# GpSimd's weight arithmetic in 128-column pieces, and w_out staged in a place of its own

## The chip, the core and the metric

The kernel runs on one core of a Trainium2 chip. The metric is the device time of one execution in microseconds (us), and a kernel's time is the median over several executions. Engines have short names in what follows: PE is TensorE, PEld its weight loads, DVE is VectorE, ACT is ScalarE, POOL is GpSimd, and SP is SyncE, which here only issues DMA transfers. Every engine works through its own instructions in a fixed order and waits where an operand or a place to write is not ready.

## The reference, cut

A linear attention without softmax, normalised per head, feeds a gated layer with a spatial product. There are 8 batches, 8 heads, 576 positions and 64 channels per head.

```python
kv  = einsum('bhsd,bhse->bhde', k, v)
out = einsum('bhsd,bhde->bhse', q, kv)
x   = out / sqrt(mean(out**2, -1) + 1e-6) * g_norm      # (B, S, 512)
h   = maximum(x @ w_in, 0);  u, v = h[..., :512], h[..., 512:]
v_n = (v - mean(v)) / sqrt(var(v) + 1e-6)
v_s = einsum('ts,bsd->btd', w_spatial, v_n) + b_spatial[None, :, None]
result = (u * v_s) @ w_out
```

## The kernel before

Operands of the large products are split into a high and a low part (XH and XL, WIH and WIL, WSH and WSL, VH and VL, GH and GL, WOH and WOL), and each product is three products: high by high, high by low, low by high (`three`, L223). One batch goes through these stages.

- Attention, a pair of heads at a time: `att_k` (K, tile `pskv`), `att_qa` and `att_qb` (Q, tiles `pso` and `pst`, the normalised result `x`), `att_t` (T, transposition into `pstr`, from which ACT writes XH and DVE writes XL). The last 64 positions of all pairs go through `pstt`. All these PSUM tiles but `pst` share three places (`ps_att`).
- `hv` (tile `psh`): the second half of x @ w_in for 128 positions, then the layer norm on ACT and DVE, which gives VH and VL. `hv_tail` does this for the last 64 positions of two batches and writes TA and TB.
- `u_unit` (tile `psu`): a 128-channel, 288-position piece of the first half of x @ w_in, written to U by ACT.
- `sp_unit` (tile `pss`): the spatial product, which DVE multiplies with U into `g` (L298). ACT writes GH and DVE writes GL.
- `out_unit` (tile `pso2`): the last product, copied out by ACT and stored.

The weights arrive as 64-bit numbers. `weight64` (L343) decodes one 128x512 piece: ACT L348, DVE L349 and L350, ACT L351 (the high part), DVE L352 and L353, then POOL L354 (a subtraction) and L355 (an addition that writes the low part). There are eight pieces of w_in and four of w_out. The spatial weights need one ACT cast and one POOL subtraction of 640 columns each (`make_ws`, L376), and their last rows need two of each per half (`make_tail`, L393). Staged pieces live in the pool `stage0` (five places), the first four in `stage1`.

The first batch, the attention of the second, all weight loads (token W) and all decodes (token C) are written in one list of tokens, PLAN. After it, batches 1 to 7 run in a loop: hv, u, spatial, out. A scheduler orders the instructions of each engine from this program order as operands come free, so that an engine's order differs from the order of the code. The attention of later batches is queued in steps (`queue`, `step`) between the units.

Of the kernel before, what the change touches and what calls it, by code (L numbers as in the profile page):

```python
# [13 lines left out]
ALU = mybir.AluOpType  # L14
AX = mybir.AxisListType

B, H, S, D = 8, 8, 576, 64
DM, FF = 512, 1024
FH = FF // 2
P = 128  # L20
# [13 lines left out]
HALF = DM // 2  # L34
NB = B
PLAN = """
N8 W L J00 D00 L W G J01 B00 C A01 L W L J02 T00 C H30 W B01 C D02 J03 H10 W C T01 L B02 C W
T02 H20 D03 H11 L L L W C L K10 B03 L C H00 T03 H21 d0 W H12 H22 b0 W H31 J11 t0 H01 D10 H13
+ J12 W C W A11 B10 K13 C H23 u00 W A12 H32 A13 H02 W u01 u31 F1 u21 u30 u10 L C B11 W C W
F2 W u20 B12 u11 H03 H33 W T11 d1 F3 S T10 T12 F0 S C C b1 C t1 W C B13 S C T13 h C C s30  # L40
s31 s11 s21 s00 s20 s01 S s10 o1 S o3 S S S S S S o0 S o2
"""


def f32(ap):
    return ap.bitcast(F32)
# [3 lines left out]
def body(ctx: ExitStack, tc, qT, kvlo, kvhi, g2, w_in, wsT, bsp, w_out, out):  # L50
    nc = tc.nc
# [12 lines left out]
    def persistent(shape, dt, name):  # L64
        return const.tile(shape, dt, name=name, tag=name)
# [4 lines left out]
    WSH = persistent([P, NC, WC], F32R, "WSH")  # L70
    WSL = persistent([P, NC, WC], F32R, "WSL")
    WTH = persistent([P, WC], F32R, "WTH")
    WTL = [persistent([P, WC], F32R, f"WTL{i}") for i in range(2)]
# [134 lines left out]
    def att_steps(b):  # L208
        st = {}

        def t2():
            att_t(b, 2, st)
            tail_a(b, st)
            tail_b(b, st)

        K = lambda p: (lambda: att_k(b, p, st))
        Q = lambda p: (lambda: att_q(b, p, st))
        T = lambda p: (lambda: att_t(b, p, st))
        return [K(0), K(1), Q(0), K(2), Q(1), T(0), K(3), Q(2), T(1), Q(3), t2, T(3),
                lambda: att_tail(b, st)]  # L220


    def three(ps, pairs):  # L223

        n = len(pairs)
        for i, (lt, rh) in enumerate(pairs):
            nc.tensor.matmul(ps, lt, rh, start=i == 0, stop=i == n - 1)  # L227

    def hl(lh, ll, rh, rl):
        return [(lh, rh), (lh, rl), (ll, rh)]  # L230
# [17 lines left out]
    def hv(b, c):  # L248
        ps = ps_ho.tile([P, 512], F32, name="psh", tag="ho")
        for k in range(NP):  # L250
            hv_k(b, c, k, ps)
        hv_end(c, ps, nc.vector)
# [12 lines left out]
    def hv_tail():  # L265
        ps = ps_ho.tile([P, 512], F32, name="psh", tag="ho")
        cols = slice(NT, NT + 2 * TAIL)
        three(ps, [m for k in range(NP) for m in
                   hl(XH[:, k, cols], XL[:, k, cols], WIH[:, k, FH:FF], WIL[:, k, FH:FF])])
        v = layer_norm(ps, nc.vector)  # L270
        for i in range(2):
            own = slice(i * TAIL, (i + 1) * TAIL)
            other = slice((1 - i) * TAIL, (2 - i) * TAIL)
            nc.scalar.copy(TA[i][own], v[own])
            nc.vector.tensor_copy(TB[i][own], v[own])
            nc.vector.tensor_tensor(TA[i][other], v[own], f32(TA[i][own]), op=ALU.subtract)

    def u_unit(b, d, j):
        ps = ps_us.tile([P, 512], F32, name="psu", tag="us")
        cols = slice(j * HS, (j + 1) * HS)  # L280
        xs = slice(b % 2 * S + j * HS, b % 2 * S + (j + 1) * HS)
        fs = slice(d * P, (d + 1) * P)
        three(ps[:, 0:HS], [m for k in range(NP) for m in
                            hl(WIH[:, k, fs], WIL[:, k, fs], XH[:, k, xs], XL[:, k, xs])])
        nc.scalar.activation(U[:, d, cols], ps[:, 0:HS], AF.Relu)  # L285

    def sp_unit(b, d, j):
# [18 lines left out]
        for src, dst in parts:  # L306
            nc.scalar.copy(GH[:, d, dst], g[:, src])  # L307
            nc.vector.tensor_tensor(GL[:, d, dst], g[:, src], f32(GH[:, d, dst]), op=ALU.subtract)

    def out_unit(b, c):  # L310
        ps = ps_ho.tile([P, 512], F32, name="pso2", tag="ho")
        cols = slice(c * P, (c + 1) * P)
        three(ps, [m for k in range(4) for m in
                   hl(GH[:, k, cols], GL[:, k, cols], WOH[:, k, :], WOL[:, k, :])])
        o = work.tile([P, DM], F32, name="o", tag="stg", bufs=2)
# [11 lines left out]


    GH = GL = WOH = WOL = None
    staging = [ExitStack(), ExitStack()]  # L330
    pools = [staging[0].enter_context(tc.tile_pool(name="stage0", bufs=5)),
             staging[1].enter_context(tc.tile_pool(name="stage1", bufs=4, side="right"))]
    staged = {}

    def stage(i, n, dt=F32):
        pool = pools[1 if i < 4 else 0]
        staged[i] = pool.tile([P, 2 * DM], dt, name="stage", tag="stage")[:, 0:n]
        return staged[i]

    def load64(src, i):  # L340
        nc.sync.dma_start(stage(i, 2 * DM, U32), src)

    def weight64(i, hi, lo):  # L343

        wide = staged.pop(i).rearrange("p (f two) -> p f two", two=2)
        w0, w1 = wide[:, :, 0], wide[:, :, 1]
        t = work.tile([P, DM], U32, name="t", tag="stg", bufs=2)
        nc.scalar.activation(f32(t), f32(w1), AF.Abs, scale=2.0 ** -112)  # L348
        nc.vector.tensor_scalar(t, t, 3, None, op0=ALU.logical_shift_left)  # L349
        nc.vector.scalar_tensor_tensor(w1, w1, 0x80000000, t, op0=ALU.bitwise_and, op1=ALU.bitwise_or)  # L350
        nc.scalar.copy(hi, f32(w1))  # L351
        nc.vector.tensor_scalar(t, w1, 0xFF800000, None, op0=ALU.bitwise_and)  # L352
        nc.vector.scalar_tensor_tensor(f32(w0), w0, 2.0 ** -52, f32(t), op0=ALU.mult, op1=ALU.mult)  # L353
        nc.gpsimd.tensor_tensor(f32(w1), f32(w1), f32(hi), op=ALU.subtract)  # L354
        nc.gpsimd.tensor_tensor(lo, f32(w1), f32(w0), op=ALU.add)  # L355

    def w_in_cols(half):
        return slice(half * FH, (half + 1) * FH)
# [14 lines left out]
    def load_ws(c, i):  # L373
        nc.sync.dma_start(stage(i, WC), wsT[c * P:(c + 1) * P, :])

    def make_ws(c, i):  # L376
        t = staged.pop(i)
        nc.scalar.copy(WSH[:, c, :], t)
        nc.gpsimd.tensor_tensor(WSL[:, c, :], t, f32(WSH[:, c, :]), op=ALU.subtract)

    def tail_rows(i):
        h0 = (1 - i) * TAIL
        return slice(i * TAIL, (i + 1) * TAIL), slice(h0, h0 + TAIL), h0, h0 + 32

    def load_tail(i, slot):

        rows, rest, h0, h1 = tail_rows(i)
        t = stage(slot, WC)
        nc.sync.dma_start(t[rows], wsT[NC * P:S, :])
        for r in (h0, h1):  # L390
            nc.sync.dma_start(t[r:r + 1], bsp)

    def make_tail(i, slot):  # L393
        rows, rest, h0, h1 = tail_rows(i)
        t = staged.pop(slot)
        nc.gpsimd.memset(f32(WTL[i][rest]), 0.0)
        nc.gpsimd.memset(f32(TB[i][rest]), 0.0)
        for r in (h0, h1):
            nc.gpsimd.memset(f32(TB[i][r:r + 1]), 1.0)
        nc.scalar.copy(WTH[rows], t[rows])  # L400
        nc.gpsimd.tensor_tensor(WTL[i][rows], t[rows], f32(WTH[rows]), op=ALU.subtract)
        for r in (h0, h1):
            nc.scalar.copy(WTL[i][r:r + 1], t[r:r + 1])
        low = WTL[i][h1:h1 + 1]
        nc.gpsimd.tensor_tensor(low, t[h1:h1 + 1], f32(low), op=ALU.subtract)


    todo = [(b, p) for b in range(B) for p in range(NP)]
# [9 lines left out]
    def ahead(n=1):  # L418
        wanted[0] += n
        issue()  # L420
# [17 lines left out]
    def enqueue(b):  # L438
        for i, s in enumerate(att_steps(b)):
            def go(i=i, s=s):  # L440
                s()
                if i in (2, 4, 7, 9):
                    ahead()
            queue.append(go)

    def step(n=1):
        for _ in range(n):
            if queue:
                queue.pop(0)()

    def spatial(b, d, j):
        nonlocal GH, GL
        if GH is None:
            staging[0].close()
            gates = ctx.enter_context(tc.tile_pool(name="gates", bufs=1))
            GH, GL = (gates.tile([P, 4, NT + 2 * TAIL], F32R, name=n, tag=n)
                      for n in ("GH", "GL"))
        sp_unit(b, d, j)
# [6 lines left out]
    loads = [lambda ld=ld, args=args, n=n: ld(*args, n) for n, (ld, mk, args) in enumerate(jobs)]  # L465
# [28 lines left out]
    for token in PLAN.split():  # L494
        do[token[0]](*map(int, token[1:]))

    for b in range(1, NB):
        for c in range(NC):
            hv(b, c)
            step()  # L500
        for d in range(4):
            if d == 3 and b % 2 == 0:
                step(len(queue))
                hv_tail()
            for j in range(2):
                u_unit(b, d, j)
                step()
        step(len(queue))
        if b + 2 < NB:
            enqueue(b + 2)  # L510
        for d in range(4):
            for j in range(2):
                sp_unit(b, d, j)
                step()
        for c in ([NC] if b % 2 else []) + list(range(NC)):
            out_unit(b, c)
            step()


_OUTS = [((B, S, DM), "float32")]  # L520
# [41 lines left out]
```

## Time and profile before

| | us |
|---|---|
| median of three runs | 553.45 (552.96 to 555.08) |
| the profiled execution, its own time | 550.85 |
| its span, first to last instruction | 549.1 |
| PE busy in the span | 524.3 |
| DVE busy | 312.6 |
| ACT busy | 220.1 |
| POOL busy | 51.8 |

The profiled execution is 2.6 us shorter than the median, so a change is worked out against the profiled execution and then carried over to the median. PE is busy nearly all the time after the first 97 us. In the first 97 us, which load and decode the weights, PE has gaps, and DVE has almost none from 20 us on. All of POOL's work lies in the first 88 us.

### The profile page before, as it was taken

What the parts mean: (1) busy time and instruction counts of PE and PEld (TensorE: products, weight loads), DVE (VectorE), ACT (ScalarE), POOL (GpSimd) and SP (SyncE); (2) the same over time, 40 slices, a digit from 0 to 9 for tenths busy, and PEclk for the clock granted to TensorE, in tenths of its full rate; (3) what the DMA queues carried; (4) which work ended last, traced back from release to release, by engine and by line L of the source; (5) the groups of instructions that cost most, each with busy time, mean ns of one, the idle gap of its engine ahead of it and who ended that gap; (6) DMA issues with size and microseconds to landing.
All of it is one profiled execution on the core that took longest, in us unless ns stands there. A gap on an engine that the chain in (4) does not pass through costs nothing.

```text
span 549.1 us, 8840 instructions
## 1 busy us (share of the span) xinstructions
PE 524.3 (95%) x3344; PEld 480.0 (87%) x3344; DVE 312.6 (57%) x871; ACT 220.1 (40%) x576; POOL 51.8 (9%) x50
## 2 busy tenths in 40 slices
PE   7787978999999999999999999999999999999996
PEld 6666966988998889988999889988999889988995
DVE  1999999813565465555364465646546456314530
ACT  3766955422434343243433344334332434123312
POOL 6356643000000000000000000000000000000000
PEclk9999899999999999999999999999999999999999
DMA  8999835111244103430333202431100200010002
GB/s 227 288 278 227 271 90 140 33 39 39 69 104 125 59 0 89 112 116 20 87 88 84 100 1 65 109 108 55 44 23 1 78 20 1 0 47 32 1 1 96
DMA packets 20034, 46.26 MB, mean 84 GB/s; under 512 B 2644, under 2 KB 3156, under 8 KB 19992
## 3 DMA queue, kind: packets, MB, share of 16 engines
q1 hardware_dynamic: 19992, 45.70, 30.0%
q8 instruction: 26, 0.43, 0.3%
q14 instruction: 16, 0.13, 0.1%
HBM read 36.25 MB, written 9.44 MB: 83 GB/s over the span
## 4 chain that ended last, share of the span: by engine, by line
PE 82%; DVE 3%; ACT 0%; issue 0%; ACTq 0%; DVEq 0%
PE pss L227 21%; PE pso L227 18%; PE psu L227 16%; PE psh L258 14%; PE pskv L110 4%; PE pso L165 4%; PE pstr L195 2%; PE psh L227 1%; PE pst L170 1%; PE pstt L203 0%; DVE stage L353 0%; DVE ss L151 0%; DVE XL L189 0%; DVE x L157 0%; DVE rh L133 0%
## 5 line engine op out<-in xcount | busy, mean ns | idle before, releaser
L227 PE MATMUL pss<-WSH,VH 128*128 128x288 f32 x256 | 78.8, 308 | 1.3 <-DVE g L298 1.3
L227 PE MATMUL psu<-XH,WIH 128*128 128x288 f32 x256 | 77.6, 303 | 0.3 <-ACT U L285 0.3
L227 PE MATMUL psu<-XL,WIH 128*128 128x288 f32 x256 | 76.1, 298 | 0.0
L227 PE MATMUL psu<-XH,WIL 128*128 128x288 f32 x256 | 76.0, 298 | 0.0
L227 PE MATMUL pss<-WSH,VL 128*128 128x288 f32 x256 | 75.5, 295 | 0.0
L227 PE MATMUL pss<-WSL,VH 128*128 128x288 f32 x256 | 75.4, 295 | 0.0
L307 ACT CAST GH<-g 128x288 fp32r<-128x288 f32 (+2 forms) x80 | 29.0, 382 | 83.3 <-DVE g L298 83.2
L227 PE MATMUL pso<-WOH,GH 128*128 128x512 f32 x144 | 58.8, 408 | 0.4 <-ACT o L320 0.4
L227 PE MATMUL pso<-WOL,GH 128*128 128x512 f32 x144 | 56.8, 395 | 0.0
L227 PE MATMUL pso<-WOH,GL 128*128 128x512 f32 x144 | 56.8, 398 | 0.0
L237 DVE BATCH_NORM_STATS2 s<-v 128x6 f32<-128x512 f32 x36 | 24.8, 692 | 52.5 <-ACT v L234 52.5
L298 DVE TENSOR_TENSOR g<-pss,U 128x288 f32<-128x288 f32 x64 | 29.1, 456 | 44.8 <-PE pss L227 44.2
L258 PE MATMUL psh<-WIH,XH 128*128 128x512 f32 x128 | 51.0, 398 | 0.5 <-ACT XH L188 0.5
L227 PEld LDWEIGHTS psu<-XH,WIH 128*128 128x128 f32 x256 | 48.8, 191 | 1.5 <-ACT U L285 0.4
L258 PE MATMUL psh<-WIL,XH 128*128 128x512 f32 x128 | 50.1, 391 | 0.0
L227 PEld LDWEIGHTS pss<-WSH,VH 128*128 128x128 f32 x256 | 48.2, 188 | 2.0 <-DVE g L298 1.5
L227 PEld LDWEIGHTS psu<-XL,WIH 128*128 128x128 f32 x256 | 48.7, 190 | 1.2
L227 PEld LDWEIGHTS psu<-XH,WIL 128*128 128x128 f32 x256 | 48.7, 190 | 0.8
L258 PE MATMUL psh<-WIH,XL 128*128 128x512 f32 x128 | 48.6, 392 | 0.2 <-DVE XL L189 0.2
L110 PE MATMUL pskv<-KV 128*128 128x128 f32 x320 | 45.6, 282 | 3.2 <-DMA KV<-kvhi 3.0
L227 PEld LDWEIGHTS pss<-WSL,VH 128*128 128x128 f32 x256 | 48.2, 188 | 0.4
L227 PEld LDWEIGHTS pss<-WSH,VL 128*128 128x128 f32 x256 | 48.0, 188 | 0.0
(100 smaller groups left out, 982.0 us busy)
## 6 DMA issues: line engine op xcount, KB each, us to landing
KV<-kvlo SPq DMA_DIRECT2D x31, 320.0 KB, 4.5
qt<-qT SPq DMA_DIRECT2D x32, 288.0 KB, 3.9
out<-o SPq DMA_DIRECT2D x32, 256.0 KB, 2.0
KV<-kvhi SPq DMA_DIRECT2D x31, 256.0 KB, 4.0
stage<-w_in SPq DMA_DIRECT2D x8, 512.0 KB, 10.3
stage<-w_out SPq DMA_DIRECT2D x4, 512.0 KB, 6.6
stage<-wsT SPq DMA_DIRECT2D x4, 320.0 KB, 12.3
out<-o SPq DMA_DIRECT2D x8, 128.0 KB, 2.3
```

What stands on the lines that cost most here:

```text
L110: nc.tensor.matmul(ps[:, 0:P], kv[:, 0, c, :], kv[:, 1, c, :], start=c == 0, stop=c == NC)
L165: nc.tensor.matmul(ps[:, c * P:(c + 1) * P], qt[:, c * P:(c + 1) * P], kvb, start=True, stop=True)
L170: nc.tensor.matmul(st["tail"][:, p * P:(p + 1) * P], qt[:, S - P:S], kvb, start=True, stop=True)
L195: nc.tensor.transpose(ps[:, c * P:(c + 1) * P], x[:, c * P:(c + 1) * P], ident)
L227: nc.tensor.matmul(ps, lt, rh, start=i == 0, stop=i == n - 1)
L237: nc.vector.bn_stats(s6, v)
L258: nc.tensor.matmul(ps, lt, rh, start=k == 0 and i == 0, stop=k == NP - 1 and i == 2)
L298: nc.vector.tensor_tensor(g, ps[:, 0:HS], U[:, d, cols], op=ALU.mult)
L307: nc.scalar.copy(GH[:, d, dst], g[:, src])
```

## The change

Every POOL subtraction and addition of the weights is cut into pieces of 128 columns (`pieces`): a 128x512 instruction becomes four, a 128x640 or 64x640 one becomes five. POOL's 32 such instructions become 136. The four pieces of w_out get staging places of their own (`stage2`, two places). PLAN loses its last four loads (W) and decodes (C) and the outputs of batch 0 (o), and batch 1 now runs its hv and u units, with the w_out loads and decodes written among them, before batch 0's outputs.

```diff
 PLAN = """
-... F2 W u20 B12 u11 H03 H33 W T11 d1 F3 S T10 T12 F0 S C C b1 C t1 W C B13 S C T13 h C C s30
-s31 s11 s21 s00 s20 s01 S s10 o1 S o3 S S S S S S o0 S o2
+... F2 u20 B12 u11 H03 H33 T11 d1 F3 S T10 T12 F0 S C C b1 C t1 B13 S T13 h s30 s31 s11 s21 s00 s20 s01 S s10
...
+    stage_out = ctx.enter_context(tc.tile_pool(name="stage2", bufs=2))
...
-        pool = pools[1 if i < 4 else 0]
+        pool = stage_out if i >= 14 else pools[1 if i < 4 else 0]
...
+    def pieces(out, a, b, op):
+        for c in range(0, out.shape[-1], P):
+            nc.gpsimd.tensor_tensor(out[:, c:c + P], a[:, c:c + P], b[:, c:c + P], op=op)
...
-        nc.gpsimd.tensor_tensor(f32(w1), f32(w1), f32(hi), op=ALU.subtract)
-        nc.gpsimd.tensor_tensor(lo, f32(w1), f32(w0), op=ALU.add)
+        pieces(f32(w1), f32(w1), f32(hi), ALU.subtract)
+        pieces(lo, f32(w1), f32(w0), ALU.add)
...
-    for b in range(1, NB):
+    def first(b):
         for c in range(NC):
             hv(b, c)
             step()
+            if b == 1 and c < 2:
+                loads.pop(0)()
...
             for j in range(2):
                 u_unit(b, d, j)
                 step()
+            if b == 1:
+                conv()
+                if loads:
+                    loads.pop(0)()
...
+    first(1)
+    last(0)
+    second(1)
+    last(1)
+    for b in range(2, NB):
+        first(b)
+        second(b)
+        last(b)
```

`second` holds the spatial units and `last` the output units. The same cut into pieces is made in `make_ws` and `make_tail`.

What the scheduler makes of it is seen in the engines' orders. First SP, where the transfers are issued, from the last w_in load on: `kvlo`, `kvhi` and `qt` are the attention's inputs (KV0_97 with qt_387 before and qt_420 after is batch 1's third pair), `wsT` the spatial weights. Before:

```order
L341 DMA stage_456<-w_in 128x1024
L374 DMA stage_469<-wsT 128x640
L99 DMA KV0_97<-kvhi 64x2x512
L97 DMA KV0_97<-kvlo 64x1280
L101 DMA qt_387<-qT 128x576
L99 DMA KV1_98<-kvhi 64x2x512
L97 DMA KV1_98<-kvlo 64x1280
L374 DMA stage_535<-wsT 128x640
```

And now:

```order
L341 DMA stage_501<-w_in 128x1024
L379 DMA stage_514<-wsT 128x640
L341 DMA stage_1313<-w_out 128x1024
L341 DMA stage_1354<-w_out 128x1024
L98 DMA KV0_97<-kvhi 64x2x512
L96 DMA KV0_97<-kvlo 64x1280
L100 DMA qt_420<-qT 128x576
L98 DMA KV1_98<-kvhi 64x2x512
L96 DMA KV1_98<-kvlo 64x1280
L379 DMA stage_580<-wsT 128x640
```

The first two w_out pieces are loaded ahead of the inputs of batch 1's last two pairs; before, they stood 23 transfers later.

Second DVE, just after the last w_in piece is decoded, among the layer norms of batch 0's first hv units (`rv`, `qv`, `v`) and the attention's norms (`rh`, `qh`, `ss`). Before:

```order
L128 RECIPROCAL qh_515<-ah_513 128x8
L133 TENSOR_TENSOR rv_680<-sv_678,qv_679 128x1
L133 TENSOR_TENSOR rv_760<-sv_758,qv_759 128x1
L134 SCALAR_TENSOR_TENSOR qv_679<-sv_678,rv_680 128x1
L134 SCALAR_TENSOR_TENSOR qv_759<-sv_758,rv_760 128x1
L133 TENSOR_TENSOR rh_516<-sh_514,qh_515 128x8
L135 SCALAR_TENSOR_TENSOR rv_680<-qv_679,rv_680 128x1
L135 SCALAR_TENSOR_TENSOR rv_760<-qv_759,rv_760 128x1
L134 SCALAR_TENSOR_TENSOR qh_515<-sh_514,rh_516 128x8
L241 TENSOR_SCALAR v_671<-v_671,mv_674,rv_680 128x512
```

And now, where L354, L355, L357 and L358 are the four DVE steps of a decode (L349, L350, L352 and L353 before):

```order
L354 TENSOR_SCALAR t_1596<-t_1596 128x512
L357 TENSOR_SCALAR t_1521<-stage_1313 128x512
L127 RECIPROCAL qv_820<-av_818 128x1
L127 RECIPROCAL qh_560<-ah_558 128x8
L132 TENSOR_TENSOR rv_735<-sv_733,qv_734 128x1
L355 SCALAR_TENSOR_TENSOR stage_1354<-stage_1354,t_1596 128x512
L150 TENSOR_REDUCE ss_606<-sq_605 128x8
L358 SCALAR_TENSOR_TENSOR stage_1313<-stage_1313,t_1521 128x512
L132 TENSOR_TENSOR rv_821<-sv_819,qv_820 128x1
L132 TENSOR_TENSOR rh_561<-sh_559,qh_560 128x8
L133 SCALAR_TENSOR_TENSOR qv_734<-sv_733,rv_735 128x1
L357 TENSOR_SCALAR t_1596<-stage_1354 128x512
```

The decodes of the first two w_out pieces now stand here; before they stood after batch 0's layer norms. The other two pieces keep about their place on DVE.

Third PE, from the end of `hv_tail` (psh_1002 before, psh_1053 now) on. Before:

```order
L227 MATMUL psh_1002<-WIL_80,XH_86 128x512
L227 MATMUL psh_1002<-WIH_79,XL_87 128x512
L110 MATMUL pskv_1195<-KV1_98 128x128 x5
L165 MATMUL pso_1238<-KVB1_96,qt_533 128x128 x4
L170 MATMUL pst_964<-KVB0_95,qt_734 128x128
L195 MATMUL pstr_1280<-ident_100,x_980 128x128 x4
L110 MATMUL pskv_1287<-KV2_99 128x128 x5
L165 MATMUL pso_1295<-KVB0_95,qt_734 128x128 x4
L170 MATMUL pst_964<-KVB1_96,qt_984 128x128
L227 MATMUL pss_1062<-WTH_83,TA0_90 128x288
```

And now, where psh_1255 and psh_1315 are batch 1's first two hv units:

```order
L226 MATMUL psh_1053<-WIL_80,XH_86 128x512
L226 MATMUL psh_1053<-WIH_79,XL_87 128x512
L109 MATMUL pskv_1228<-KV1_98 128x128 x5
L257 MATMUL psh_1255<-WIL_80,XH_86 128x512
L257 MATMUL psh_1255<-WIH_79,XL_87 128x512
L257 MATMUL psh_1255<-WIH_79,XH_86 128x512
L257 MATMUL psh_1255<-WIL_80,XH_86 128x512
L257 MATMUL psh_1255<-WIH_79,XL_87 128x512
L257 MATMUL psh_1255<-WIH_79,XH_86 128x512
L257 MATMUL psh_1255<-WIL_80,XH_86 128x512
L257 MATMUL psh_1255<-WIH_79,XL_87 128x512
L164 MATMUL pso_1287<-KVB1_96,qt_578 128x128 x4
```

Two more hv units of batch 1 (psh_1315, psh_1356) stand between these and the first product with TA, and a fourth before the third spatial unit.

## Rows read from the trace of the kernel before

**Rows 1.** The page, parts 1 and 2: PE's busy time and its 40 slices.
```profile
PE 524.3 (95%) x3344; PEld 480.0 (87%) x3344; DVE 312.6 (57%) x871; ACT 220.1 (40%) x576; POOL 51.8 (9%) x50
PE   7787978999999999999999999999999999999996
```

**Rows 2.** Busy by stretch: length, PE, PEld, DVE, ACT, POOL, PEclk, DMA share, GB/s.
```profile
46.00:67.00 21.00, 17.11 (x122) 16.46 (x121) 20.83 (x60) 17.22 (x50) 15.07 (x10) 0.92 0.91 253
67.00:97.00 30.00, 23.69 (x162) 21.60 (x161) 29.61 (x73) 17.03 (x50) 11.72 (x8) 0.94 0.47 126
97.00:545.00 448.00, 447.55 (x2864) 411.12 (x2862) 228.11 (x674) 158.31 (x368) 0.00 (x0) 1.00 0.20 56
```

**Rows 3.** PE's waits, 46 to 100 us: us in total, times, longest.
```profile
PE pstt L203 <- DVE x L157: 3.6, 1, 3.6
PE pso L165 <- DVE x L157: 2.6, 1, 2.6
...
```

**Rows 4.** DVE in order of time: start us, us, instruction.
```profile
18.15 0.69 DVE L353 SCALAR_TENSOR_TENSOR stage<-stage,t 128x512 f32<-128x512 uint32 x1
18.76 1.26 DVE L133 TENSOR_TENSOR rh<-sh,qh 128x8 f32<-128x8 f32 x1
...
48.64 1.50 DVE L353 SCALAR_TENSOR_TENSOR stage<-stage,t 128x512 f32<-128x512 uint32 x1
...
53.02 0.16 DVE L133 TENSOR_TENSOR rh<-sh,qh 128x8 f32<-128x8 f32 x1
...
87.28 0.77 DVE L133 TENSOR_TENSOR rh<-sh,qh 128x8 f32<-128x8 f32 x1
```

**Rows 5.** POOL in order of time: start us, us, instruction.
```profile
0.74 0.20 POOL L425 MEMSET KVB<- 128x128 f32 x1 [0.29 <-POOLq L552]
2.71 0.52 POOL L397 MEMSET TB<- 64x512 f32 x1
...
18.45 1.55 POOL L354 TENSOR_TENSOR stage<-stage,WIH 128x512 f32<-128x512 f32 x1 [7.59 <-ACT WIH L351]
...
48.31 1.29 POOL L354 TENSOR_TENSOR stage<-stage,WIH 128x512 f32<-128x512 f32 x1 [0.76 <-issue]
...
65.24 1.56 POOL L405 TENSOR_TENSOR WTL<-stage,WTL 1x640 fp32r<-1x640 f32 x1 [0.97 <-ACT WTL L403]
...
86.99 1.04 POOL L355 TENSOR_TENSOR WOL<-stage 128x512 fp32r<-128x512 f32 x1
```

**Rows 6.** DVE again: the bounds of a stretch, and the decodes of w_out.
```profile
39.33 0.41 DVE L349 TENSOR_SCALAR t<-t 128x512 uint32<-128x512 uint32 x1
...
67.00 0.68 DVE L263 TENSOR_TENSOR VL<-v,VH 128x512 fp32r<-128x512 f32 x1
...
70.67 0.41 DVE L349 TENSOR_SCALAR t<-t 128x512 uint32<-128x512 uint32 x1
...
72.55 0.16 DVE L127 TENSOR_SCALAR ah<-ss 128x8 f32<-128x8 f32 x1
...
73.07 1.69 DVE L353 SCALAR_TENSOR_TENSOR stage<-stage,t 128x512 f32<-128x512 uint32 x1
...
76.95 1.26 DVE L349 TENSOR_SCALAR t<-t 128x512 uint32<-128x512 uint32 x1
```

**Rows 7.** PE in order of time: a u unit's start, batch 2's first K, the last wait.
```profile
65.05 0.30 PE L227 MATMUL psu<-XH,WIH 128*128 128x288 f32 x1
...
66.64 1.27 PE L110 MATMUL pskv<-KV 128*128 128x128 f32 x10
...
96.09 0.40 PE L227 MATMUL pss<-WSH,VH 128*128 128x288 f32 x1 [1.28 <-DVE g L298]
```

**Rows 8.** Three w_out loads issued from 60.23 us: issue to landing.
```profile
L341 SPq DMA_DIRECT2D stage<-w_out x3: 355/371/385, 60.2 to 61.2; - x3
...
DMA to landing us min/median/max: 5.0/5.9/6.8
```

**Rows 9.** ACT in order of time: a cast that waits for a load.
```profile
53.72 0.72 ACT L378 CAST WSH<-stage 128x640 fp32r<-128x640 f32 x1 [2.19 <-DMA stage<-wsT]
```

More of the change, by code (lines that the diff above doesn't have):

```diff
@@ L36 @@
 PLAN = """
[L37 to L40, printed above, removed]
-s31 s11 s21 s00 s20 s01 S s10 o1 S o3 S S S S S S o0 S o2
+N8 W L J00 D00 L W G J01 B00 C A01 L W L J02 T00 C H30 W B01 C D02 J03 H10 W C T01 L B02 C W T02
+H20 D03 H11 L L L W C L K10 B03 L C H00 T03 H21 d0 W H12 H22 b0 W H31 J11 t0 H01 D10 H13 + J12 W
+C W A11 B10 K13 C H23 u00 W A12 H32 A13 H02 W u01 u31 F1 u21 u30 u10 L C B11 W C F2 u20 B12 u11
+H03 H33 T11 d1 F3 S T10 T12 F0 S C C b1 C t1 B13 S T13 h s30 s31 s11 s21 s00 s20 s01 S s10
 """
@@ L378, in make_ws @@
         nc.scalar.copy(WSH[:, c, :], t)
-        nc.gpsimd.tensor_tensor(WSL[:, c, :], t, f32(WSH[:, c, :]), op=ALU.subtract)
+        pieces(WSL[:, c, :], t, f32(WSH[:, c, :]), ALU.subtract)
     def tail_rows(i):
@@ L400, in make_tail @@
         nc.scalar.copy(WTH[rows], t[rows])
-        nc.gpsimd.tensor_tensor(WTL[i][rows], t[rows], f32(WTH[rows]), op=ALU.subtract)
+        pieces(WTL[i][rows], t[rows], f32(WTH[rows]), ALU.subtract)
         for r in (h0, h1):
@@ L404, in make_tail @@
         low = WTL[i][h1:h1 + 1]
-        nc.gpsimd.tensor_tensor(low, t[h1:h1 + 1], f32(low), op=ALU.subtract)
+        pieces(low, t[h1:h1 + 1], f32(low), ALU.subtract)
     todo = [(b, p) for b in range(B) for p in range(NP)]
@@ L510, in body, with second @@
             enqueue(b + 2)
+    def second(b):
         for d in range(4):
@@ L514, in body, with last @@
                 step()
+    def last(b):
         for c in ([NC] if b % 2 else []) + list(range(NC)):
@@ L550 @@
     arrays = {n: np.ascontiguousarray(a) for n, a in arrays.items()}
-    nc = bacc.Bacc("TRN2", target_bir_lowering=False, num_devices=1)
+    nc = bacc.Bacc("TRN2", target_bir_lowering=False, num_devices=1,
+                   dynamic_dma_scratch_size=1024)
     args = [nc.dram_tensor(n, a.shape, mybir.dt.from_np(a.dtype), kind="ExternalInput").ap()
```

## The prediction, made before the changed kernel ran

> **What bounds the kernel now.** I read the page first: PE is busy for 95% of the span, and the slices in which it is not are all near the start [rows 1]. Busy time by stretch puts an edge on that: from 97 us on PE idles for half a microsecond in 448, so nothing there can be won but by less PE work, and the change leaves PE's work as it is. Between 46 and 97 us PE idles 3.9 + 6.3 = 10.2 us, and its clock is granted at 0.92 and 0.94 of full speed, which costs another 1.7 + 1.8 us [rows 2]. The clock fell to the lower level, 1.2 GHz, after PE's two long waits. The change can win some of these 13.7 us or add to them; what happens before 97 us moves all that follows by the same amount.
>
> The waits name who is late: DVE, for `x` in the two longest [rows 3] and for `g` in the last [rows 7]. DVE is busy 20.83 of 21 and 29.61 of 30 us there [rows 2], so it is the bound. But busy is not working: L353 takes 0.69 us at 18.15 and 1.50 us at 48.64, a 128x8 product 1.26 us at 18.76 and 0.77 at 87.28, where the same form takes 0.16 at 53.02 [rows 4]. The instruction of 18.76 ends at 20.02; POOL's of 18.45 ends at 20.00 [rows 5]. All 29 DVE instructions between these two times that are longer than the shortest of their form, 21.9 us in sum, end in that way with a POOL instruction. So DVE's instructions with two operands in SBUF, and its `TENSOR_SCALAR`, stand still while POOL reads, and those that read PSUM don't. The reverse holds as well: POOL's subtraction of 128x512 takes 1.29 us at 48.31 and 1.55 at 18.45, the addition 1.04 at its shortest [rows 5].
>
> **The change part by part.** *Where PE is first held.* `ps_att` has three places, so batch 2's first K (`pskv`, at 66.64 before [rows 7]) needs the `x` of batch 1's third Q to be read. Before, the DVE rows up to that `x` run from 39.33 to 67.00 [rows 6]: 27.7 us, of which 12 stalls are 9.9. Now two w_out decodes stand among them. A decode's four DVE steps take 1.88 us (70.67 to 72.55), two 3.7; their four stalls were 1.00 for the first (73.07: 1.69 instead of 0.69), 0.36, 0.73 and 0.85 (76.95: 1.26 instead of 0.41) [rows 6], 2.9 in sum. With stalls as long as before, that `x` is there at 67.0 + 3.7 + 2.9 = 73.6.
>
> *What the pieces give back.* A piece holds DVE for a time that the trace does not show. A quarter of 1.04 is 0.26 us. From above: POOL's fill of 128 columns takes 0.20 us and of 512 columns 0.52 [rows 5], so 0.09 is paid for each instruction; 0.95 / 4 + 0.09 gives 0.33. From below: the instruction of 18.76 needs 0.16 of its own and ended 0.02 after POOL, so DVE was let go some 0.15 us before POOL's end; 0.33 less 0.15 is 0.18. I take 0.26, the middle and the quarter. How many pieces meet DVE I took from nine POOL jobs, 48.31 to 65.24 [rows 5], that would be 43 pieces: laid beside DVE's rows one by one, with DVE's waiting instruction let in after each piece, about 20 of them meet one that must wait; the rest fall on PSUM readers. Twenty by 0.26 is 5.2 us, where the stalls were 6.9. With 0.22 the walk gives 4.0, with 0.30 it gives 6.4: a short row of two-operand instructions is now held several times, for less. So a quarter of the 9.9 + 2.9 = 12.8 us is won, 3.2, and the `x` comes at 73.6 - 3.2 = 70.4.
>
> The Trainium skill ("GPSIMD Engine Reference", § 3.1 Elementwise) speaks against the cut: it has about 2.6 cycles an element for two inputs, and a dispatch on each instruction, so the sum of POOL's holds would not fall. By it the `x` would stay near 73.6, the third rival below; its estimate of 0.28 us for 128 columns at 1.2 GHz, four of which are 1.1, agrees with the 1.04 of the row.
>
> *What PE then has behind it.* K at 70.4 instead of 66.64, and one u unit less done by then (twelve products, 65.05 to 66.64: 1.6 us [rows 7]): PE is 3.8 + 1.6 = 5.4 us later than before at the same amount of work.
>
> *What PE wins behind it.* Before, it lost 6.3 us of waits and 1.8 of clock between 67 and 97 us [rows 2], the longest wait 3.6 before `pstt` [rows 3] and the last 1.28 at 96.09 [rows 7]; and each of some eight restarts costs about 0.1 (0.40 us for the first product, 0.30 in a full row [rows 7]), 1.0 with the weights' part. Together 9.1. Now two of four decodes are behind it, and four hv units of batch 1, twelve products each, 2.8 us a unit, stand behind `hv_tail`, ready long before: between `hv_tail` and the first `g` PE has 15.6 us of work where DVE needs 13.8; before it had 7.4. So I let all waits go, and leave one stretch at the lower clock after the wait for `x`, 1.5 us, since that wait is as long as those that led to it before. Won: 9.1 - 1.5 = 7.6.
>
> *Sum.* 5.4 - 7.6 = 2.2 us less: 550.85 - 2.2 = 548.65 for the profiled execution, and with the 2.6 us by which the median lies above it, **551.3 us**.
>
> *Edits at nothing.* The two early loads take (6.8 - 5.0 + 1.0) / 2 = 1.4 us each where they stand in a row [rows 8], so all transfers behind land 2.8 us later; ACT's cast of `wsT` already waited 2.19 us for one [rows 9]. This lies under the 3.8 us that PE is late anyway; if the `x` came sooner, it would be the next to be late, at 66.64 + 2.8 = 69.4. The last w_in piece's low part now has 31 POOL pieces ahead of it, from 42.5 us until PE reads it at 64.6, 0.71 us for each: covered twice over. Batch 0's outputs, moved behind batch 1's u units, keep PE's order of the last 1849 products, so nothing behind 97 us is charged. New waits on the two places of `stage2` stand on SP, with later batches' inputs behind them; these have tens of microseconds.
>
> **The rivals.** *Each stall falls to a quarter.* If DVE, once let in, kept POOL out until its row is through, 12.8 us of stalls would be 3.2 and the `x` no gate; ACT's late casts then set 69.4, one microsecond less: 550.3, and 548.8 without the stretch at the lower clock. For it: POOL is held too, its subtraction takes 1.29 in one place and 1.55 in another [rows 5]. Against: DVE's next instruction starts within 0.1 us of the last, and POOL gets in between. The Trainium skill ("SBUF — State Buffer", § Who interferes with whom) says that whoever issues first has the shared ports for the whole instruction and the other blocks fully; that agrees with the ends at 20.00 and 20.02, and lets both in by turns, and so by itself bears out the forecast more than this rival.
>
> *The cut gives nothing.* `x` at 73.6, 3.2 later than forecast: 554.5.
>
> *Slower.* A fixed cost in each POOL instruction stretches the holds. The walk grows by 2.4 us for 0.08 us of hold: 0.35 us makes 7.9 of the 6.9, all stalls 14.7, the `x` at 75.5 and the time 556.4. This is where it turns; 0.38 makes 558.0. For it: the 0.09 us of the fills, above 0.33. Against: the early release.
>
> *The early decodes cost PE nothing,* because PE's work is not held at K, as other work is ready in the scheduler's order: 550.85 - 7.6 + 2.6 = 545.9.
>
> **How the numbers follow.** Forecast 0.40 (its own range 549.5 to 553.5), quarter of the stalls 0.22, nothing from the cut 0.15, longer holds 0.13, no gate 0.10. About 0.5%, 2.8 us, is what a measurement of this kernel can tell: faster means below 550.7, slower above 556.2. Faster: 0.10 of the forecast's, 0.17 of the second's and the last's 0.10, 0.37. Slower: 0.13 and 0.04 of the third's, 0.17. The same: 0.46. The range, 546.5 to 557.0, leaves out half of the last case and about half of the longer holds.
>
> **What would show it right or wrong.** In the profile after: POOL's pieces at about 0.3 us; DVE's excess over its shortest forms at three quarters of 21.9 plus what stays of w_out's; batch 2's first K near 70 us, waiting for DVE `x` L156; one stretch at the lower clock there, and from about 72 us no waits of PE. A K at 67 us makes the first term wrong; waits of several microseconds at `pstt` or the first `g` make the gain wrong; pieces over 0.4 us make it slower.

## The result, and the profile after

| | before | after |
|---|---|---|
| median of four runs each, us | 553.97 (552.96 to 555.08) | 545.93 (545.72 to 549.45) |
| the profiled execution, its own time | 550.85 | 546.0 |
| its span | 549.1 | 544.2 |

The ratio of the times is 0.9869, with a 95% interval of 0.9824 to 0.9914: the change makes the kernel 1.3% faster. The forecast of 551.3 us had the sign and about a quarter of the size (2.2 us of 8.0), and the time lies 0.6 us below the low end of the range. The profiled executions are 4.9 us apart; what follows reads these 4.9 us, not the whole 8.0.

Busy time by stretch, of the kernel after (columns as in [rows 2]):

```profile
46.00:67.00 21.00, 16.23 (x91) 15.07 (x90) 17.73 (x54) 12.04 (x35) 21.00 (x44) 0.77 0.95 216
67.00:97.00 30.00, 29.50 (x198) 27.17 (x199) 23.90 (x62) 18.03 (x45) 19.86 (x41) 1.00 0.36 99
97.00:540.00 443.00, 442.51 (x2852) 407.57 (x2850) 227.10 (x679) 158.85 (x370) 0.00 (x0) 1.00 0.21 58
```

PE's idle time from 67 to 97 us went from 6.3 us to 0.5, and its clock there from 0.94 to 1.00. Ahead of 67 us PE is worse off than it was: 4.8 us idle instead of 3.9, and the clock at 0.77 instead of 0.92. DVE, which had almost no free time between 46 and 97 us before, has 3.3 + 6.1 us now. POOL is the one without a gap there: 21.00 of 21.00 until 67 us.

PE's waits, 46 to 100 us, after (us in total, times, longest), which answer to [rows 3]:

```profile
PE psu L226 <- ACT U L284: 3.4, 2, 2.9
PE pso L164 <- ACT KVB L114: 0.7, 1, 0.7
PE psu L226 <- POOL WIL L346: 0.7, 1, 0.7
PE pst L169 <- DMA qt<-qT: 0.4, 1, 0.4
```

The two long waits for DVE's `x` are gone. What PE waits longest for now is U, which ACT writes. PE in order of time shows where that stands (start us, us, instruction, wait ahead of it):

```profile
66.92 0.40 PE L226 MATMUL psu<-XH,WIH 128*128 128x288 f32 x1 [2.87 <-ACT U L284]
...
68.61 1.27 PE L109 MATMUL pskv<-KV 128*128 128x128 f32 x10
...
72.39 0.40 PE L226 MATMUL psu<-XH,WIH 128*128 128x288 f32 x1 [0.50 <-ACT U L284]
```

The middle row is batch 2's first K, the step that the prediction put at 70.4 us ([rows 7] have it at 66.64 before). The last row is PE's last wait ahead of 100 us; before, it was at 96.09.

DVE after, in order of time; in [rows 4] a 128x8 product (L133 there, L132 here) took 1.26 us where it was held:

```profile
51.08 0.42 DVE L132 TENSOR_TENSOR rv<-sv,qv 128x1 f32<-128x1 f32 x1
51.43 0.15 DVE L132 TENSOR_TENSOR rh<-sh,qh 128x8 f32<-128x8 f32 x1
51.50 0.43 DVE L133 SCALAR_TENSOR_TENSOR qv<-sv,rv 128x1 f32<-128x1 f32 x1
```

The first and the last row are stalls: 0.28 us each (0.42 for what takes 0.14). The stalls are shorter now and lie closer together. Over the whole trace I took each DVE instruction's excess over the shortest of its form, where it is above 0.12 us: 57 instructions after with 13.0 us in all, 0.23 each, against 29 before with 22.5. POOL after, in order of time:

```profile
50.55 2.46 POOL L346 TENSOR_TENSOR stage<-stage,WIH 128x128 f32<-128x128 f32 x4
...
81.79 1.47 POOL L346 TENSOR_TENSOR WOL<-stage 128x128 fp32r<-128x128 f32 x4
```

The four pieces of an addition take 1.47 us at the shortest, where the whole one took 1.04 [rows 5]. The four pieces of a subtraction take 2.46 beside a busy DVE, where the whole one took 1.29 to 1.55.

### The profile page after: what moved, and what is told of

The parts are those of the page before. It is cut to its first block, busy times and chain, and to the rows that moved or that the text cites. A ratio compares the mean times of both kernels' runs of the same rounds, so it can differ in the third digit from the quotient of the medians.

```text
span 544.2 us, 8938 instructions
## 1 busy us (share of the span) xinstructions
PE 524.4 (96%) x3344; PEld 481.7 (89%) x3344; DVE 302.3 (56%) x871; ACT 220.1 (40%) x576; POOL 76.7 (14%) x154
## 4 chain that ended last, share of the span: by engine, by line
PE 86%; DMA 10%; ACT 2%; SPq 1%; DVE 1%; POOL 0%; issue 0%; ACTq 0%
PE pss L226 22%; PE pso L226 19%; PE psu L226 17%; PE psh L257 14%; PE pskv L109 5%; DMA stage<-wsT 4%; PE pso L164 4%; DMA stage<-w_in 4%; PE pstr L194 2%; PE psh L226 2%; DMA KV<-kvlo 1%; PE pst L169 1%; PE pstt L202 1%; SPq L98 0%; SPq L96 0%; POOL WIL L346 0%
## 5 line engine op out<-in xcount | busy, mean ns | idle before, releaser
L109 PEld LDWEIGHTS pskv<-KV 128*128 128x128 f32 x320 | 43.0, 202 | 6.0 <-DMA KV<-kvlo 3.0
```

Source lines behind the costliest of these rows:

```text
L109: nc.tensor.matmul(ps[:, 0:P], kv[:, 0, c, :], kv[:, 1, c, :], start=c == 0, stop=c == NC)
```

## The experiments

Most of these kernels hold the order of every engine by a table, so that two of them in one order differ in one thing. Two more things go with the order of after in all of them: w_out's own staging places, and a setting where the program is built (`dynamic_dma_scratch_size=1024`) that the cut diff above does not show. No run separates these two from the order. The table has the ranks of an engine's instructions in the order of the code, and each instruction is made to be issued behind the one before it:

```python
for a, z in zip(ranks, ranks[1:]):
    tc.add_manual_dep(ours[z], ours[a].name, mybir.DependencyInfo(
        mybir.DependencyClass.NoSync, mybir.DependencyReason.DATA), reason="order")
```

### Pieces and order, one without the other

The pieces in the order of before, and the order of after with whole instructions:

```diff
-        nc.gpsimd.tensor_tensor(lo, f32(w1), f32(w0), op=ALU.add)
+        pieces(lo, f32(w1), f32(w0), ALU.add)       # order of before held
...
-        for c in range(0, out.shape[-1], P):
-            nc.gpsimd.tensor_tensor(out[:, c:c + P], a[:, c:c + P], b[:, c:c + P], op=op)
+        nc.gpsimd.tensor_tensor(out, a, b, op=op)   # order of after held
```

> The kernel before with POOL's 32 subtractions and additions cut into pieces of 128 columns, and nothing else: every engine's order is held as it was before, SP's too. Theory 1 (the pieces bring the gain: DVE is the bound until 97 us and its stalls shrink, 22 us in sum before, 13 us after the change): 547 to 550 us, DVE's stalls at 12 to 15 us. Theory 2 (the gain is the new order, which gives PE work while DVE is late): 552.5 to 555 us, POOL's longer work (51.8 us before, 76.7 after) eating what DVE wins.

> The changed kernel with POOL's instructions whole, as before, and every engine's order held as in the changed kernel. Theory 1 (pieces): the x that batch 2's first K waits for comes at 73 to 74 us instead of 67.8, and the time is 550 to 554 us. Theory 2 (order): 545 to 548 us, since PE has work enough behind hv_tail whenever DVE is late. If both parts are needed together it is between, 548 to 550.

| ratio to before (95%) | order of before | order of after |
|---|---|---|
| whole instructions | 1 | 1.0003 (0.9982 to 1.0024) |
| pieces of 128 | 0.9929 (0.9909 to 0.9949) | 0.9869 (0.9824 to 0.9914) |

Theory 1 holds for the first part: the pieces bring 0.7% by themselves, 548.44 us. The order brings nothing by itself, 551.9 us beside 552.6 for before on the same chip. With the pieces it adds about 0.6%, as far as intervals that overlap by a hair can tell. So the two parts hardly are a sum, and theory 2, the order by itself, is out as it stood.

In the order of before, with pieces, batch 2's first K comes at 62.52 us instead of 66.64, and then PE still waits as it did before. PE's waits, 46 to 100 us, of this kernel:

```profile
PE pstt L203 <- DVE x L157: 2.5, 1, 2.5
PE psu L227 <- POOL WIL L346: 1.9, 1, 1.9
PE psu L227 <- ACT U L285: 1.3, 2, 1.1
PE pss L227 <- DVE g L298: 1.3, 1, 1.3
```

In the order of after with whole instructions that K comes late, and nothing is lost behind it. PE in order of time, and the DVE rows from the decode step that stood at 39.33 us before [rows 6] to the `x` that K waits for:

```profile
73.65 1.38 PE L109 MATMUL pskv<-KV 128*128 128x128 f32 x10 [1.17 <-DVE x L156]
```

```profile
38.93 0.42 DVE L353 TENSOR_SCALAR t<-t 128x512 uint32<-128x512 uint32 x1
...
72.93 0.67 DVE L156 TENSOR_TENSOR x<-pso,rh 128x512 f32<-128x512 f32 x1
```

K waits for the `x` that the prediction named, and at the time it gave for stalls as long as before, 73.6 us. In the profiles in this order the span is that K plus nearly the same rest:

| order of after, with | first K of batch 2, us | span, us | span less K |
|---|---|---|---|
| whole instructions | 73.65 | 549.5 | 475.9 |
| pieces of 256 | 70.42 | 546.5 | 476.1 |
| pieces of 128 (after) | 68.61 | 544.2 | 475.6 |
| the same, order held by the table | 68.10 | 543.7 | 475.6 |

In the order of before the same difference is 482.5 (549.1 less 66.64) and 484.1 with pieces (546.6 less 62.52). What the new order buys is these 7 to 8.5 us behind K; what it costs is a later K. With whole instructions the two cancel.

> The changed kernel itself, its order held by the same table as in the kernels above: a control for the table, and a second look at the point that both theories speak of. If the table changes nothing: 545 to 547.5 us. If the span is batch 2's first K plus a fixed 475 us, as in the five kernels in this order so far (474.7 to 476.1, the kernel with pieces of 64 columns aside), K and span agree to 0.5 us again wherever K falls; and a K that is later than 68.6 us comes with a later landing of the spatial weights' or KV loads, not with longer stalls of DVE, if the transfers are the last gate.

The control took 545.33 us (543.23 to 549.47), ratio 0.9868 (0.983 to 0.9906): the table itself costs nothing that shows.

### The size of a piece

The order of after, with pieces of 256 and of 64 columns:

```diff
-        for c in range(0, out.shape[-1], P):
+        for c in range(0, out.shape[-1], 256):    # or 64
...                                              # the slices as wide
```

> The changed kernel with pieces of 256 columns instead of 128, every engine's order held as in the changed kernel. Whole instructions in this order gave x for batch 2's first K at 73.7 us, 551.9 us in all, pieces of 128 gave 67.8 and 545.9. If it is the length of a hold that counts: DVE's stalls between 26.5 (whole) and 13.0 (128 columns), about 18 us, K near 70 us and 547 to 549 us. Rival: POOL's own length counts as well (it is busy all the time from 20 to 67 us with pieces of 128, and PE waited 0.7 us for a low part of w_in): with 72 pieces instead of 136 POOL is shorter by some 10 us, the stagings come free earlier, and the time is the same as with 128 or less, 544 to 546.5 us.

> The changed kernel with pieces of 64 columns, every engine's order held as in the changed kernel. If the length of a hold alone counts: stalls below 10 us and 544 to 546 us. Rival (a cost for each POOL instruction, so that POOL, which is busy all the time from 20 to 67 us, gets longer and hands on low parts and staging places later): POOL above 90 us busy, PE waits of several us for WIL or for the spatial weights, 548 to 556 us.

Pieces of 256 gave 547.72 us (0.9896, 0.9879 to 0.9912), with K at 70.42: as the first theory had it, but for the stalls, 21 us instead of about 18. Pieces of 64 gave 557.42 us, slower than before (1.0082, 1.0058 to 1.0105): as the rival had it. The first lines of four pages, whole, 256, 128, 64:

```profile
PE 523.3 (95%) x3344; PEld 480.0 (87%) x3344; DVE 314.0 (57%) x871; ACT 220.4 (40%) x576; POOL 50.6 (9%) x50
```

```profile
PE 524.2 (96%) x3344; PEld 481.0 (88%) x3344; DVE 309.0 (57%) x871; ACT 220.2 (40%) x576; POOL 62.2 (11%) x90
```

```profile
PE 524.4 (96%) x3344; PEld 481.7 (89%) x3344; DVE 302.3 (56%) x871; ACT 220.1 (40%) x576; POOL 76.7 (14%) x154
```

```profile
PE 528.5 (94%) x3344; PEld 484.9 (87%) x3344; DVE 300.0 (54%) x871; ACT 219.7 (39%) x576; POOL 97.9 (18%) x290
```

DVE's busy time falls from 314.0 to 300.0 and POOL's rises from 50.6 to 97.9. DVE's stalls above 0.12 us are 30 of 0.88 us with whole instructions, 49 of 0.43 with 256 columns, and 57 of 0.23 with 128. From 256 to 128 the length of a stall halves and the number hardly grows. The stalls lose 5.4 us from whole to 256 and 8.1 from 256 to 128, but K moves by 3.2 and 1.8 us: with 256 it still waits for its `x`, with 128 for something else, which the next section looks for. With 64 columns it is POOL that is late. PE's waits of that kernel, 46 to 100 us:

```profile
PE psu L226 <- POOL WIL L346: 11.6, 3, 5.3
PE pskv L109 <- DVE x L156: 2.1, 1, 2.1
```

Its K comes at 77.83 us, and behind it PE waits another 4.5 us, until 103.38, so that the span of 559.3 is K plus 481.5 and not 476. This profile is of the longest of the kernel's six executions, 561.13 us, 3.7 above their median, so its waits can be longer than those of the others. The slower rival of the prediction is real, one step further down.

### What the K of after waits for

The chain of waits of after, in order of time (start us, us, what), runs through the loads of the spatial weights:

```profile
38.87 11.79 DMA stage<-wsT
50.66 0.02 issue
50.68 0.03 SPq L379
50.71 0.03 issue
50.74 11.54 DMA stage<-wsT
62.28 0.02 issue
62.30 0.73 ACT WSH L383
```

A load of 320 KB takes 11.5 us there, with the DMA share at 0.95 from 46 to 67 us. ACT of after, in order of time, shows what stands behind the last of them:

```profile
62.30 0.73 ACT L383 CAST WSH<-stage 128x640 fp32r<-128x640 f32 x1 [2.48 <-DMA stage<-wsT]
62.94 0.59 ACT L233 ACTIVATE v<-psh 128x512 f32<-128x512 f32 x1
63.43 0.71 ACT L405 CAST WTH<-stage 64x640 fp32r<-64x640 f32 x1
64.16 1.47 ACT L408 CAST WTL<-stage 1x640 fp32r<-1x640 f32 x2
...
66.45 0.42 ACT L284 ACTIVATE U<-psu 128x288 f32<-128x288 f32 x1
```

PE's unit of 66.92 waits for the U of 66.45, and K stands right behind that unit. Theory A: the transfers are the last gate. Rival: POOL, which has almost no gap from 20 to 67 us. I took half the bytes from the early w_out loads, and, apart from that, a part of POOL's work:

```diff
-        load64(w_out[k * P:(k + 1) * P, :], i)
+        t = stage(i, 2 * DM, U32)
+        if k < 2:
+            nc.gpsimd.memset(f32(t), 0.0)
+        nc.sync.dma_start(t[0:P // 2 if k < 2 else P], w_out[k * P:k * P + (P // 2 if k < 2 else P), :])
...
+        if i < 14:
             pieces(f32(w1), f32(w1), f32(hi), ALU.subtract)
```

> The changed kernel in its own order, with half the rows left out of the first two w_out loads (256 KB each instead of 512 KB; two POOL fills at about 12 to 18 us, where POOL is idle, write the rest of the two places). Theory A (the transfers are the last gate: batch 2's first K stands at 68.6 us behind U's activation, that behind the casts on ACT, and the last cast of the spatial weights waits until 62.3 us for its load): that load lands 1.5 to 2 us earlier, K comes at 66.5 to 67.5 us, and the time falls by 1 to 2 us, to 544 to 545. Rival (POOL is the gate, busy all the time from 20 to 67 us): no change, 545.5 to 546.5 us.

> The changed kernel in its own order, with POOL's subtractions for w_out left out (16 of its 136 pieces, 5 of them ahead of 61 us, some 2.5 us of POOL time there, 4 us by 65 us; w_out's low part is then another number). Theory A (transfers are the last gate): no change, 545.5 to 546.5 us. Rival (POOL's queue is the gate; its holds on DVE count as well): K 2 to 3 us earlier and 543 to 544 us.

ACT and PE in order of time, first with half the bytes, then without the subtractions:

```profile
59.60 0.72 ACT L386 CAST WSH<-stage 128x640 fp32r<-128x640 f32 x1
```

```profile
65.89 1.27 PE L109 MATMUL pskv<-KV 128*128 128x128 f32 x10
```

```profile
64.07 0.72 ACT L384 CAST WSH<-stage 128x640 fp32r<-128x640 f32 x1 [1.95 <-DMA stage<-wsT]
```

```profile
71.72 1.46 PE L109 MATMUL pskv<-KV 128*128 128x128 f32 x10
```

In the profile with half the bytes the last cast comes 2.7 us earlier and waits for no load, K comes 2.7 us earlier, and the execution takes 542.88 us. Its six executions reach from that to 548.91, however, with a median of 546.58 (ratio 0.9869, 0.9835 to 0.9903), so the times don't confirm the 544 to 545. Without the subtractions POOL is busy 17.89 of 21 us instead of 21.00, and K is not earlier but later, behind a load that was issued and landed later (issued at 52.79 us, in the control at 50.65); the median is 547.13 (0.988, 0.985 to 0.9909). That is against the rival, though one profile with a later load does not refute it. Cast and K are 7.65 us apart there: PE's unit ahead of K took 3.0 us at the lower clock (0.50 granted from 70 to 71.7 us), 1.7 in after. The control tells the same from the other side: its cast stands at 61.79 and its K at 68.10, a distance of 6.31 us, as in after (62.30 and 68.61) and with half the bytes (59.60 and 65.89, 6.29). Where the last load lands, K follows. That K hangs on the last load is shown by these traces; what it is worth in the median is not, since executions of one kernel differ by more.

Then ACT's own queue. The six casts of the last rows, 2.2 us a half, stand ahead of U; I moved them behind it, in the table alone:

```diff
-sv WSH v WTH WTL WTL sh ... U ... U ... XH ... VH sv WTH WTL WTL sh U ... XH U XH
+sv WSH v sh ... U ... U ... XH ... VH sv WTH WTL WTL sh U ... XH U XH WTH WTL WTL
```

> The changed kernel with one thing moved in its order: on ACT the three casts of each half of the spatial weights' last rows (2.2 us a half) stand behind U's activations and the sums of squares instead of ahead of them. PE waited 2.9 us for U until 66.9 us and 0.5 at 72.4, and those casts stand right ahead of U there. If what is late at that point is ACT's own queue: U at 64 to 65 us, batch 2's first K at 66 to 67 us, 544 to 545 us. Rival (the x for that K is late by itself): K at 68 to 69 us and no change, 545.5 to 546.5; should the low parts of the last rows then be late for the first product that reads them, 547 or more.

ACT and PE in order of time:

```profile
62.96 0.73 ACT L383 CAST WSH<-stage 128x640 fp32r<-128x640 f32 x1 [2.62 <-DMA stage<-wsT]
...
64.86 0.42 ACT L284 ACTIVATE U<-psu 128x288 f32<-128x288 f32 x1
```

```profile
67.77 1.38 PE L109 MATMUL pskv<-KV 128*128 128x128 f32 x10 [0.59 <-DVE x L156]
```

The load landed 0.7 us later than in after, U comes 1.6 us earlier, and now K waits for its `x` again, so that the 66 to 67 us expected for it are missed by 0.8. The cast and K are 4.8 us apart instead of 6.3: ACT's casts behind the last load are a part of what holds K, and the `x` stands close behind them. The median is 544.63 us (543.74 to 545.48), ratio 0.9839 (0.9816 to 0.9863), the shortest of this study. Its interval overlaps those of after and of the control, so it beats the kernel before; that it beats the changed one is not shown.

### The w_out loads put off

`last_load` is the last load of the spatial weights and their bias:

```diff
+        with tc.issue_after(last_load[0].ins):
             load64(w_out[k * P:(k + 1) * P, :], i)
```

> The changed kernel with all w_out loads queued on SP behind the last load of the spatial weights; the scheduler then puts all four w_out decodes behind batch 0's layer norms and attention. Theory A (the two early loads, 1 MB in a stretch where the transfers are busy all the time, delay the spatial weights, and that is the last thing PE waits for at 66.9 us; their early decodes take DVE and POOL time as well): the spatial weights land 3 us earlier, batch 2's first K comes at 64 to 66 us, and the time is 542 to 545 us. Theory B (what the early decode costs there it gives back behind 70 us, since DVE has then less to do): 545 to 547 us, with new PE waits between 75 and 97 us.

> As the kernel with late w_out loads, and with six staging places in stage0 instead of five, so that the second load of the spatial weights is issued 10 us earlier. If places are what holds the spatial weights back: another 1 to 2 us below the kernel with late loads alone. If it is the transfers, which are busy anyway: the same within 0.5 us.

Here the scheduler made a new order. The last spatial cast comes at 59.28 us, 3.0 earlier than in after, as theory A said, and K comes at 68.92, no earlier. ACT and PE in order of time:

```profile
59.28 0.73 ACT L386 CAST WSH<-stage 128x640 fp32r<-128x640 f32 x1 [1.60 <-DMA stage<-wsT]
...
62.98 0.73 ACT L408 CAST WTH<-stage 64x640 fp32r<-64x640 f32 x1 [2.11 <-DMA stage<-wsT]
63.61 0.40 ACT L284 ACTIVATE U<-psu 128x288 f32<-128x288 f32 x1
64.03 1.47 ACT L411 CAST WTL<-stage 1x640 fp32r<-1x640 f32 x2
```

```profile
64.06 0.40 PE L226 MATMUL psu<-XH,WIH 128*128 128x288 f32 x1 [3.12 <-ACT U L284]
...
68.92 1.28 PE L109 MATMUL pskv<-KV 128*128 128x128 f32 x10
```

The cast of the last rows now waits for its load, ahead of the U that PE waits for. PE goes on at 64.06, 2.9 us earlier than in after. But this order has two u units ahead of K, not one, and much of them ran at the lower clock (0.50 granted from 66 to 68 us), so its K can't be laid beside the others. PE's idle time from 46 to 67 us is 8.1 us, 4.8 in after, and 4.1 of it is one wait for DVE's `x`. The median is 548.85 us (0.9909, 0.9875 to 0.9943), with six staging places, in yet another order, 548.3 (0.9906, 0.9886 to 0.9926). The medians miss the times of both theories. What the early loads cost by themselves these two kernels can't tell, since their orders changed with the loads; that more places gain nothing fits transfers that are busy anyway.

### What the scheduler makes of each part

The pieces alone and the new list alone, with the order left to the scheduler:

> The kernel before with the pieces of 128 columns, with the scheduler free to make a new order of it. If the order made from the pieces matters little, within 1 us of the same pieces in the order of before. Theory 1: 547 to 550 us; theory 2: 552 to 556 us.

> The changed kernel with POOL's instructions whole and the scheduler free to make a new order of it (the list of tokens, the two places for w_out and the order of batch 1 as in the changed kernel). Theory 1 (pieces bring the gain): 550 to 555 us. Theory 2 (order): 545 to 548 us.

They took 551.35 us (0.9967, 0.9937 to 0.9998) and 554.45 us (1.002, 0.9999 to 1.0042). The pieces in a new order lose about half of the 0.7% that they gain in the old one. That is some 0.4% by order alone, with intervals that overlap a little, and as large as most of the effects looked for. Without a held order the experiment above could hardly have been read.

## Why the prediction was right or wrong

**What bounds the kernel** was right. Time is made and lost ahead of 97 us, DVE is late there, and it is late because POOL holds it: with shorter holds and nothing else changed, the old order gains 0.7%. One reading went too far. Not all 29 stalls end with a POOL instruction: the 128x8 forms end 0.02 us behind one, the 128x512 forms 0.3 to 0.6 behind it (L353 of 48.64 at 50.14, POOL's of 48.31 at 49.60), as instructions that still have most of their own 0.69 us ahead of them when they are let in.

**The first gate** was right: batch 2's first K behind one `x`, 73.6 us with stalls as before. The kernel with whole instructions in the new order shows K at 73.65, waiting for that `x`.

**What the pieces give back** was sized too small: K came at 68.61 instead of 70.4. The length of a hold was right (0.26 taken, 0.23 measured). The step that failed is the start of the sum at 39.33 us, as if the stalls ahead of it stayed. The two kernels in the order of after show it at the DVE instruction with which the sum begins, L353 in the whole one and L354 in after:

```profile
36.52 0.47 DVE L354 TENSOR_SCALAR t<-t 128x512 uint32<-128x512 uint32 x1 [0.22 <-ACT t L353]
...
67.11 0.67 DVE L156 TENSOR_TENSOR x<-pso,rh 128x512 f32<-128x512 f32 x1
```

With whole instructions it stood at 38.93: DVE is 2.4 us ahead where the sum begins, and the sum had nothing for that. From there to the `x` it wins another 3.4 (72.93 - 67.11, less 2.4), where the sum had 3.2, and that with a halt in between, for ACT's `v` behind the late cast:

```profile
63.56 0.69 DVE L236 BATCH_NORM_STATS2 s<-v 128x6 f32<-128x512 f32 x1 [2.06 <-ACT v L233]
```

The `x` is through at 67.78, and K was held to 68.61 by the gate that the prediction had put next, ACT behind the late loads, at 69.4.

**What PE wins behind K**: 7.6 forecast, 8.5 measured (3.6 us late at K, 68.61 - 66.64 + 1.6, and 4.9 us shorter in the end). The reason was right: hv units of batch 1 fill what DVE needs, and from 72.4 us on PE does not wait. The term for a stretch at the lower clock behind K was wrong: the clock is 1.00 from 67 us on, and the lower stretches lie ahead of K (0.77 from 46 to 67 us), where PE waits for U in the end anyway, 2.87 us until 66.92.

**The carry to the median** was the largest miss. I added 2.6 us because the profiled execution of before lay that far below its median. The one of after lies at its median, 546.0 and 545.93. Of the 5.4 us between forecast and result 1.8 are K, 0.9 what lies behind it, and 2.7 this carry. The profile of before was a lucky draw: of the 66 other executions of that kernel on record one is shorter than 550.85 us. So the traces account for 4.9 of the 8.0 us; what the longer executions of before do is open, since none of them was profiled.

**The rivals.** Each stall to a quarter: in the order of after, whole against pieces, the stalls fell from 10.7 to 5.2 us up to 46 us, from 6.7 to 5.1 from 46 to 67, where the prediction had walked along POOL's jobs and expected three quarters, and from 9.0 to 2.8 behind; a half in sum, not a quarter. The cut gives nothing: no; the cut is what the change lives by. The time of the case without a gate, 545.9, is the measured one by chance: the gate is there, at 68.61. Longer holds: not at 128 columns, but the cost for each instruction is there, and at 64 it decides.

The rule of the Trainium skill ("GPSIMD Engine Reference", § 3.1 Elementwise) that spoke against the cut is half borne out. POOL's own time grows with each instruction, as its dispatch on each would have it: four pieces take 1.47 us for 1.04. That the holds on DVE would not get less, which the prediction drew from it, is refuted by the 26.5 and 13.0 us of stalls in one order. The one on the shared ports ("SBUF — State Buffer", § Who interferes with whom), by which the loser blocks for a whole instruction of the other, agrees with a stall that halves with the piece: 0.88, 0.43, 0.23 us.

## What to carry to other kernels

Where two engines block each other for whole instructions, cut the instructions of the one with slack, and stop before the fixed cost of each makes that engine the late one: here 128 columns gain and 64 lose. A sum that starts in the middle of a program has to ask what the change does to the time at which it starts, and the difference between one profiled execution and the median should not be carried over as if it belonged to the kernel. Two parts of a change are told apart only where the scheduler's order is held, since its answer to a new instruction length was worth about 0.4% here.

## What the runs showed that I had not expected

Each POOL instruction more cost 0.16 to 0.29 us: 40 more made POOL 11.6 us busier (50.6 to 62.2), 64 more 14.5, 136 more 21.2, waits for DVE included. A 320 KB load takes 11.5 us from issue to landing while the transfers are busy, and the time at which the last one lands differs by 2.3 us between two profiles with equal loads in the same order (casts at 61.79 and 64.07, the second without POOL's subtractions); 2.1 us of that is that the load was issued later.
